# Two-pair attention stack on one core: key weights on SyncE's queue, two tiles centred by ScalarE, five packed tiles instead of seven

## The chip, the cores and the metric

The kernel runs on one core of one Trainium2 chip. The metric is the device time of one execution in microseconds (us); the median of three executions of the kernel before is 408.18 us (407.64 to 408.44). A profiled execution, the one that the trace describes, took 409.25 us, of which 407.40 us lie between its first and its last instruction (the span).

## The reference

Four residual layers run over 2048 rows of 512 features, 32 heads of 16 features each, in bf16. Layers A and B alternate, with the same weights both times: A, B, A, B.

```python
phi = lambda t: jnp.where(t > 0, t + 1, jnp.exp(t)) + 1e-6      # layer A
kv  = einsum("bhsd,bhse->bhde", phi(k), v);  z = sum over s of phi(k)
o   = (phi(q) @ kv) / (phi(q) . z + 1e-6)
scores = q @ k.T * Dh ** -0.5                                    # layer B
mask   = (i - j >= 0) & (i - j < 256)                            # each row sees itself and 255 before it
o      = softmax(where(mask, scores, -1e9)) @ v
x = x + A(layernorm(x)); x = x + B(layernorm(x)); and both again
```

## The kernel before

The rows are cut into T = 16 tiles of 128, kept in SBUF from the first load to the last store. The engines: PE is TensorE, ACT ScalarE, DVE VectorE, POOL GpSimd, SP SyncE (it only issues DMAs).

A tile is normalised in `norm`: `stats` and `aggr` (mean and variance) on DVE, `eps` and `pow` (the variance to the power of -0.5, into `rs`) on POOL, then `xn` on DVE subtracts the mean and multiplies by `rs`. The result is transposed into `XQ`, for the first five tiles by PE (`T`, then a copy `Te` out of PSUM by ACT or DVE), for the others by a transposing DMA of SP. From the transposed tile PE makes keys (`k`, four matmuls of 512 columns in two halves `h`, each with two of the four row blocks of the weights `wA[:, :, 512:1024]`) and, for pairs of tiles, queries (`q`). `phi` finishes keys and queries: ACT takes the exponential (`E`), DVE clips it (`E1`), and then either DVE adds one and takes the larger straight from PSUM (`phi`, L451 in the profile), or ACT makes a copy with the one added (`R`, L446) and DVE takes the larger from SBUF (`mx`, L449). In the first layer PE also sums `g`, the product of the normalised tile with its keys.

Layer B works per tile j with keys `kB` against 256 + 64 query columns in blocks of 64 keys: `b_scores` (`s`, L710 on PE, L720 on ACT: the exponential of 128 x 1024 scores) and, for the 64 columns at the window's far end, `b_far` (L826 on PE, two exponentials of 128 x 1024 each, L835, and two masks `mf`, L806 on POOL or L807 on DVE). A packed tile (`PACK`) starts its 256 columns 32 later and takes the two remaining corners of 32 columns together in `b_edge` (L779 on PE, two exponentials of 128 x 512 each, L788, one more mask `ma` on DVE, L794), so that it computes 288 columns instead of 320. Then `pv` (L856) multiplies by the values, and `rcp`, `div` finish the rows.

The order is not made by a scheduler at run time. `place` unpacks `TABLE`, which holds the order of all operations, the engine of those that two engines can do (copies out of PSUM, masks `mf`, stores), and the PSUM bank of each result. Every engine plays its own list in that order and waits on semaphores where an operand comes from another engine, so an instruction that waits holds up all behind it on its engine. PE starts with matmuls on zeros (nine in `play`, seven `fill` in the table) until the first data are there. The first x tiles come on SP's queue, the key weights on ACT's.

## Time and profile before

| | |
|---|---|
| median of 3 runs | 408.18 us (407.64 to 408.44) |
| profiled execution | 409.25 us, span 407.40 us, mean granted TensorE clock 0.998 |
| busy, share of the span | PE 95%, ACT 86%, DVE 86%, POOL 31% |
| first layer (keys of all tiles) | to about 44 us |
| second layer | about 50 to 225 us |
| third layer's sums and queries | about 225 to 256 us |
| fourth layer | about 250 to 395 us, last store behind it |

A PE that is busy 95% of the span is not one that could give no more: its matmuls are pipelined, and the time of one covers its latency. What it waits for is read from the gaps between the starts of its instructions, and from the chain of work that ended last, which the page follows back from the last instruction.

### The profile page before, as it was taken

The numbers are of one execution on the slowest core, as the hardware profiler recorded it, in microseconds if no ns is written. First come the engines' busy times: TensorE is split into PE (matmuls) and PEld (weight loads), VectorE is DVE, ScalarE is ACT, GpSimd is POOL, SyncE is SP. The second block draws the span as 40 slices with busy tenths as digits, with TensorE's granted clock in tenths as the row PEclk, the third lists the DMA queues.
The fourth block names the chain that finished last, engine by engine and source line by source line (L and its number), as shares of the span: only waits on it lengthen the run. The fifth ranks groups of instructions, "written<-read, shape, count | busy, mean of one in ns | idle before, by whom it ended". The sixth has DMA issues, their size and how long they took to land.

```text
span 407.4 us, 17007 instructions
## 1 busy us (share of the span) xinstructions
PE 386.1 (95%) x7394; PEld 255.7 (63%) x7466; DVE 349.3 (86%) x818; ACT 350.4 (86%) x447; POOL 125.8 (31%) x215
## 2 busy tenths in 40 slices
PE   7999999999999999999999999999999989998996
PEld 3644576667475567565656767676656756666674
DVE  5998899999999899888877799998899689777674
ACT  2843559999999999999999368999999999999992
POOL 3588752122243142331602122301203241320130
PEclk9999999999999999999999999999999999999999
DMA  7546324443233425553222100562324433572551
GB/s 253 138 113 163 98 42 107 101 101 81 68 101 78 91 82 121 80 108 80 77 49 56 27 2 2 121 122 69 80 55 101 119 89 68 111 142 77 85 148 40
DMA packets 66986, 37.15 MB, mean 91 GB/s; under 512 B 47648, under 2 KB 62368, under 8 KB 66912
## 3 DMA queue, kind: packets, MB, share of 16 engines
q1 hardware_dynamic: 66080, 34.75, 36.8%
q8 instruction: 59, 0.97, 1.1%
q0 software_dynamic: 288, 0.79, 0.5%
q10 hardware_dynamic: 544, 0.52, 0.4%
q14 instruction: 15, 0.12, 0.1%
HBM read 6.29 MB, written 2.10 MB: 21 GB/s over the span
## 4 chain that ended last, share of the span: by engine, by line
PE 54%; ACT 21%; DVE 14%; issue 5%; DMA 3%; POOL 1%; SPq 1%; POOLq 0%; DVEq 0%
PE ps L420 19%; ACT pb L720 16%; PE ps L856 11%; PE ps L434 8%; PE ps L710 6%; PE ps L480 4%; DVE stats L374 2%; ACT pb L835 2%; PE ps L524 2%; DVE XQ L625 2%; ACT vp L720 2%; DMA xres<-in_A_x_dram 1%; DVE xres L638 1%; DVE vp L451 1%; PE ps L826 1%
## 5 line engine op out<-in xcount | busy, mean ns | idle before, releaser
L720 ACT ACTIVATE pb<-ps 128x1024 bf16<-128x1024 f32 (+2 forms) x216 | 199.4, 1021 | 3.6 <-PE ps L710 2.4
L856 PEld LDWEIGHTS ps<-vB,pb 128*128 128x128 bf16 x2560 | 78.6, 96 | 11.4 <-issue 3.6
L856 PE MATMUL ps<-vB,pb 128*128 128x34 bf16 x2560 | 84.4, 177 | 0.3
L806 POOL TENSOR_SCALAR_AFFINE_SELECT pb<-pb 128x1024 bf16<-128x1024 bf16 x33 | 37.9, 1150 | 106.0 <-DVE pb L807 40.1
L434 PE MATMUL ps<-xT,wBp 128*128 128x128 bf16 x1024 | 69.6, 219 | 0.9 <-ACT pb L720 0.5
L434 PEld LDWEIGHTS ps<-xT,wBp 128*128 128x128 bf16 x1024 | 59.2, 98 | 13.3 <-issue 4.7
L444 ACT ACTIVATE tE<-ps 128x512 bf16<-128x512 f32 x64 | 37.8, 606 | 24.4 <-PE ps L420 9.9
L379 POOL TENSOR_SCALAR ve<-mv 128x1 f32<-128x1 f32 x63 | 16.4, 260 | 130.3 <-DVE mv L375 128.4
L710 PE MATMUL ps<-XQ,kB 32*128 32x256 bf16 (+3 forms) x992 | 48.1, 267 | 3.0 <-DVE o L869 0.5
L420 PE MATMUL ps<-wA,XQ 128*128 128x512 bf16 x175 | 45.3, 379 | 1.7 <-issue 0.5
L638 DVE TENSOR_TENSOR xres<-ps,xres 128x512 bf16<-128x512 f32 x63 | 42.8, 683 | 4.7 <-PE ps L420 4.2
L374 DVE BATCH_NORM_STATS2 stats<-xres 128x6 f32<-128x512 bf16 x64 | 43.2, 681 | 4.0 <-DMA xres<-in_A_x_dram 3.5
L728 DVE TENSOR_TENSOR pb<-pb,tri 128x512 bf16<-128x512 bf16 (+1 forms) x108 | 43.0, 407 | 3.8 <-ACT pb L720 2.9
L380 POOL TENSOR_TENSOR rs<-ve,negh 128x1 f32<-128x1 f32 x64 | 40.3, 630 | 7.6 <-DVE ve L377 2.4
L835 ACT ACTIVATE pb<-ps 128x1024 bf16<-128x1024 f32 x40 | 39.4, 1054 | 1.1 <-PE ps L826 1.1
L480 PE MATMUL ps<-XQ,wA 128*128 128x256 bf16 x256 | 34.1, 273 | 0.4 <-ACT pb L720 0.4
L710 PEld LDWEIGHTS ps<-XQ,kB 32*128 32x128 bf16 x992 | 15.0, 92 | 28.8 <-ACT pb L720 7.6
L420 PE MATMUL ps<-M,XQ 128*128 128x512 bf16 x113 | 30.5, 380 | 2.4 <-issue 0.6
L420 PE MATMUL ps<-wBv,xT 128*128 128x512 bf16 x109 | 30.3, 380 | 2.3 <-issue 1.4
L420 PE MATMUL ps<-wBo,oT 128*128 128x512 bf16 x107 | 28.9, 380 | 2.6 <-DVE tE L447 0.7
L869 DVE TENSOR_TENSOR o<-ps,rc 128x256 bf16<-128x256 f32 x64 | 27.0, 423 | 1.6
L480 PEld LDWEIGHTS ps<-XQ,wA 128*128 128x128 bf16 x256 | 23.6, 98 | 7.5 <-ACT pb L720 0.8
(132 smaller groups left out, 543.8 us busy)
## 6 DMA issues: line engine op xcount, KB each, us to landing
vB<-vS SPq DMA_DIRECT2D x64, 136.0 KB, 2.5
kB<-vp SPq DMA_DIRECT2D x60, 128.0 KB, 2.1
out_dram<-xres SPq DMA_DIRECT2D x9, 128.0 KB, 2.2
wA<-in_A_wqkv_dram SPq DMA_DIRECT2D x2, 512.0 KB, 5.5
xres<-in_A_x_dram SPq DMA_DIRECT2D x2, 512.0 KB, 4.0
pb<-in_B_wqkv_dram SPq DMA_DIRECT2D x1, 1024.0 KB, 6.6
xres<-in_A_x_dram SPq DMA_DIRECT2D x3, 256.0 KB, 5.5
out_dram<-xres POOLq DMA_DIRECT2D x6, 128.0 KB, 2.6
```

Source lines behind the costliest of these rows:

```text
L374: self.on("DVE", "stats", lambda e: e.bn_stats(K.stats[:, t, :], x()), key, dve(512), rd=rd, wr=[("stats", t)], **held)
L380: self.pow = self.on("POOL", "pow", lambda e: e.tensor_tensor(K.rs[:, t, :], K.ve[:, t, :], K.negh[:], ALU.pow), key + 0.03, (640, 690), r ...
L420: m = e.matmul(K.ps(ps), lhs(c), rhs(c), start=c == 0 and not whole, stop=c == 3)
L434: m = e.matmul(K.ps(ps)[:, f * P:(f + 1) * P], w(c, f), xT(c), start=c == 0, stop=c == 3)
L480: m = e.matmul(K.ps(ps)[:, 256 * h:256 * h + 256], K.wA[:, c, f * P:(f + 1) * P], xT(c), start=c == 0, stop=c == 3)
L638: self.on("DVE", "res", lambda e: e.tensor_tensor(K.xres[:, t, :], K.ps(po), K.xres[:, t, :], ALU.add), key, dve(512), rd=[("xres", t)], w ...
L710: m = e.matmul(K.ps(ps[gq])[:, ns * i:ns * i + ns], K.kB[rows, j % 4, 2 * f + b, :, :], K.XQ[rows, f, q:q + ns], start=True, stop=True, ti ...
L720: return e.activation(out(2 * h, 2, ns), i, ACT.Exp, bias=0.0, scale=0.25)
L728: return e.tensor_tensor(x, x, K.tri[:, 0, sh:64].unsqueeze(1).unsqueeze(1).to_broadcast([P, 4, n, 64 - sh]), ALU.mult)
L806: return e.affine_select(out=x, in_=x, compare_op=ALU.is_ge, fill=0.0, base=-2, pattern=[[0, 16], [-2, 64]], channel_multiplier=1)
L835: return e.activation(far(h), i, ACT.Exp, bias=0.0, scale=0.25)
L856: m = e.matmul(K.ps(ps)[:, 34 * u:34 * u + 34], K.P((b // 2) % rp)[:, gq, f, o:o + P], K.vB[:, (b // 2) % 4, b % 2, r, :], start=i == 0, s ...
```

## The change

It does seven things.

1. The two halves of the key weights (`wAk0`, `wAk1`, 256 KB each) are loaded by SP, between the loads of x; ACT issues one small DMA of 1 x 4 x 128 elements in their place, whose completion SP waits for ahead of the first `kd` (the DMAs that fill `kB` in layer B).
2. Tiles 0 and 1 (`CENTRED`) are centred by ACT (`xc`: mean minus x) without waiting for `rs`. PE transposes the centred tile in two halves, each copied out of PSUM with its sign turned, and makes the keys from it; `rs` enters as the scale of `E` and of `R`. The normalised tiles are still made by DVE, and `XQ` of these two tiles now comes by transposing DMAs of SP.
3. The keys of tiles 0 to 7 of the first layer (`KEYS_BY_ACT`) are finished with `R` on ACT and `mx` on DVE instead of `phi` on DVE.
4. Five tiles of the fourth layer are packed instead of seven: tiles 7 and 8 now go through `b_far`.
5. `TABLE` is a new one: order, engines and banks. Beside what the edits ask for, nine more of the 56 masks `mf` are POOL's (44 instead of 35), ACT has three copies of values (`ve`) instead of five, and single copies (`bke`, `bve`, `bqe`, `sc`, `ge`) change engine; the copies out of PSUM of the transposed tiles 3 and 4 are DVE's.
6. POOL's constants (masks, spreading matrices, reordered weights) come later in the first layer, behind more of the `eps` and `pow`.
7. The x tiles 8 to 15 are loaded behind the transposes of tiles 0 and 1.

```diff
-PACK = {3: (7, 8, 9, 10, 11, 12, 13, )}
+PACK = {3: (9, 10, 11, 12, 13, )}
+CENTRED = (0, 1)
+KEYS_BY_ACT = (0, 1, 2, 3, 4, 5, 6, 7)
...
-        seq += [xs(0, 1), xs(1, 2), w("wAq", "wA", "A_wqkv", 0, 512), xs(2, 4), xs(4, 6), xs(6, 8), xs(8, 12)]
+        def wk(h):
+            return ("wAk%d" % h, lambda e: e.dma_start(K.wA[:, 2 * h:2 * h + 2, 512:1024], ...), 262144, [("wAk", h)])
+        seq += [xs(0, 1), wk(0), wk(1), xs(1, 2), w("wAq", "wA", "A_wqkv", 0, 512), xs(2, 4), xs(4, 6), xs(6, 8), xs(8, 12)]
...
+        if centred:
+            self.on("ACT", "xc", lambda e: e.activation(K.xn[:, t, :], x(), ACT.Identity, bias=K.mv[:, t, 0:1], scale=-1.0), ...)
+            for h in range(2):
+                half = Tile(1, K.cls)
+                ...  # two transposes of K.xn, 128 columns each
+                self.pe("T", put, key + 0.018 + 0.0001 * h, 2, 128, rd=[("xn", t), ("ident",)], ps=[half])
+                self.either("Te", ... ACT.Copy, scale=-1.0 ... wr=[("xT", t, h)] + ([("xT", t)] if h else []), ps=[half])
+            by_pe = False
...
-    def phi(self, ps, out, wr, key, ring, near=False, after=()):
+    def phi(self, ps, out, wr, key, ring, near=False, after=(), row=None):
+        scale = lambda: dict(scale=K.rs[:, row, :]) if row is not None else {}
+        own = [("rs", row)] if row is not None else []
...
+        xT = (lambda c: K.xT[:, t, c, :]) if centred else (lambda c: K.XQ[:, c, t * P:(t + 1) * P])
+        self.phi(ps, lambda: K.pk[:, t, :], [("pk", t)], key + 0.1, 0, near=t in KEYS_BY_ACT and key < 150, row=t if centred else None)
...
-                    e.wait_ge(wsem, 1)
-                    for h in range(2):
-                        e.dma_start(self.wA[:, 2 * h:2 * h + 2, 512:1024], ...).then_inc(ksem[h], 16)
+                    e.dma_start(self.kB[0:1, 3, 0:4, :, :]..., self.A_wqkv...[0:1, :, 0:128]).then_inc(tsem, 16)
```

The new order is best seen at three places. The first is the head of SP's queue; `xres` is x, `wA` with 128x2x512 is a half of the key weights, `wA` with 128x4x512 the query weights, `pb` the weights of layer B. Before:

```order
L294 DMA xres<-in_A_x_dram 128x512 x2
L294 DMA xres<-in_A_x_dram 128x2x512 x3
L297 DMA wA<-in_A_wqkv_dram 128x4x512
L294 DMA xres<-in_A_x_dram 128x4x512 x2
L389 DMA_TRANSPOSE XQ<-vp 128x4x128 x2
L297 DMA pb<-in_B_wqkv_dram 128x4x1024
```

And now:

```order
L297 DMA xres<-in_A_x_dram 128x512 x2
L297 DMA xres<-in_A_x_dram 128x2x512 x2
L303 DMA wA<-in_A_wqkv_dram 128x2x512 x2
L297 DMA xres<-in_A_x_dram 128x2x512
L300 DMA wA<-in_A_wqkv_dram 128x4x512
L410 DMA_TRANSPOSE XQ<-vp 128x4x128 x2
L297 DMA xres<-in_A_x_dram 128x4x512 x2
```

Both key halves stand behind the loads of tiles 0 to 5, and the last two x loads moved behind two transposes, which belong to tiles 0 and 1. The second place is the head of PE's list, where `kB` stands for the matmuls on zeros, `ident` for transposes and `wA` with 128x512 for keys. Before:

```order
L277 MATMUL ps<-kB 128x512 x4
L395 MATMUL ps<-ident,vp 128x128 x4
L277 MATMUL ps<-kB 128x512
L395 MATMUL ps<-ident,vp 128x128 x4
L277 MATMUL ps<-kB 128x512
L420 MATMUL ps<-wA,XQ 128x512 x4
L395 MATMUL ps<-ident,vp 128x128 x4
L420 MATMUL ps<-wA,XQ 128x512 x8
```

And now:

```order
L280 MATMUL ps<-kB 128x512 x4
L395 MATMUL ps<-ident,xn 128x128 x8
L280 MATMUL ps<-kB 128x512 x2
L441 MATMUL ps<-wA,xT 128x512 x4
L416 MATMUL ps<-ident,vp 128x128 x4
L441 MATMUL ps<-wA,xT 128x512 x4
L416 MATMUL ps<-ident,vp 128x128 x4
L441 MATMUL ps<-wA,XQ 128x512 x2
```

The transposes of both centred tiles now stand together ahead of the keys, and read what ACT wrote (`xn`), not what DVE wrote (`vp`). The first four key matmuls are the first halves of both tiles. The third place is ACT's list in the fourth layer, around the exponentials of the far columns of tiles 7 and 8 (128x8x2x32 for a packed tile, 128x8x2x64 for another). Before:

```order
L720 ACTIVATE pb<-ps 128x2x2x256 x8
L788 ACTIVATE vp<-ps 128x8x2x32 x2
L835 ACTIVATE pb<-ps 128x8x2x64 x2
L720 ACTIVATE pb<-ps 128x2x2x256 x6
L835 ACTIVATE pb<-ps 128x8x2x64 x2
L720 ACTIVATE vp<-ps 128x2x2x256 x6
L720 ACTIVATE pb<-ps 128x2x2x256 x2
L720 ACTIVATE vp<-ps 128x2x2x256 x2
L788 ACTIVATE pb<-ps 128x8x2x32 x2
```

And now:

```order
L743 ACTIVATE pb<-ps 128x2x2x256 x8
L858 ACTIVATE vp<-ps 128x8x2x64 x2
L858 ACTIVATE pb<-ps 128x8x2x64 x2
L743 ACTIVATE pb<-ps 128x2x2x256 x6
L858 ACTIVATE pb<-ps 128x8x2x64 x2
L743 ACTIVATE vp<-ps 128x2x2x256 x6
L743 ACTIVATE pb<-ps 128x2x2x256 x2
L743 ACTIVATE vp<-ps 128x2x2x256 x2
L858 ACTIVATE pb<-ps 128x8x2x64 x2
```

Nothing changed places there; two pairs of exponentials became twice as long.

## The prediction

> **What bounds the kernel now.** I read the page's busy times, then the busy times in stretches of 10 us, then the chain of waits in order of time, then the engines' timelines where the change works. In the table by stretches, the columns are the stretch, its length, and the busy time of PE, PEld, DVE, ACT and POOL with counts, then clock, DMA share and GB/s:

> ```profile
> PE 386.1 (95%) x7394; PEld 255.7 (63%) x7466; DVE 349.3 (86%) x818; ACT 350.4 (86%) x447; POOL 125.8 (31%) x215
> 0.00:10.00 10.00, 7.89 (x32) 3.06 (x33) 5.41 (x15) 2.48 (x3) 3.27 (x14) 1.00 0.78 253
> 20.00:30.00 10.00, 9.89 (x65) 4.84 (x64) 9.92 (x30) 5.12 (x9) 8.31 (x17) 1.00 0.48 120
> 160.00:170.00 10.00, 9.78 (x213) 6.63 (x212) 8.71 (x23) 9.61 (x12) 1.70 (x4) 1.00 0.61 84
> 370.00:380.00 10.00, 9.01 (x303) 7.37 (x300) 7.14 (x20) 9.85 (x13) 0.00 (x0) 1.00 0.37 85
> ```

> PE and a second engine are full nearly everywhere, and the second changes: DVE in the first layer (9.92 of 10 at 20 to 30 us, ACT only 5.12), ACT later (9.85 at 370 to 380, with PE at 9.01). So one microsecond of ACT work is nearly free in the first layer and nearly a microsecond of time in the last. The chain of waits says the same (start, length, what):

> ```profile
> 1.72 5.19 DMA xres<-in_A_x_dram
> 27.72 0.58 DVE vp L451
> 28.35 1.04 PE ps L420 x4
> 342.08 3.77 ACT pb L720 x4
> ```

> Until 28.3 us the chain runs through the load of tiles 2 and 3, which ends at 6.91, and then mostly through DVE; from there PE and ACT carry it.

> **First layer, start.** PE's timeline (start, length, what, and the idle time before it):

> ```profile
> 6.77 0.40 PE L395 MATMUL ps<-ident,vp 128*128 128x128 bf16 x4
> 8.21 0.40 PE L395 MATMUL ps<-ident,vp 128*128 128x128 bf16 x4 [0.81 <-DVE vp L381]
> 8.65 1.24 PE L420 MATMUL ps<-wA,XQ 128*128 128x512 bf16 x4
> 9.73 0.39 PE L395 MATMUL ps<-ident,vp 128*128 128x128 bf16 x4
> 9.96 1.89 PE L420 MATMUL ps<-wA,XQ 128*128 128x512 bf16 x8
> 11.68 0.39 PE L395 MATMUL ps<-ident,vp 128*128 128x128 bf16 x4
> ```

> The matmuls on zeros end at 6.77 in both kernels. Then PE transposes tile 0, and waits for DVE to normalise tile 1, which stood behind `stats` of tile 2, that is, behind the load that ended at 6.93; the keys begin at 8.65. Start to start, four transposes take 0.23 (9.73 to 9.96) and eight key matmuls with no wait 1.72 (9.96 to 11.68), 0.215 each. In the new order, 6.77 is followed by eight transposes (0.46) and two matmuls on zeros (0.43), so keys could begin at 7.66, **1.0 earlier**. Three things must be there by then:

> ```profile
> 2.89 0.69 DVE L374 BATCH_NORM_STATS2 stats<-xres 128x6 f32<-128x512 bf16 x1 [1.69 <-DMA xres<-in_A_x_dram]
> 4.62 0.18 DVE L375 BATCH_NORM_AGGREGATE mv<-stats 128x2 f32<-128x6 f32 x1
> 7.21 0.60 ACT L402 ACTIVATE XQ<-ps 128x512 bf16<-128x512 bf16 x1 [3.68 <-PE ps L395]
> L407 ACT ACTIVATE oT<-ps 128x256 bf16<-128x256 bf16 x2 | 0.8, 384 | 3.2 <-PE ps L894 3.2
> L446 ACT ACTIVATE XQ<-ps,one 128x512 bf16<-128x512 f32 x12 | 8.1, 693 | 0.1
> ```

> Centred tiles: the means of both tiles are ready at 4.80 (4.62 + 0.18); two passes of about 0.69 on ACT (`xc` has the operands of `R`, L446) end at 5.5 to 6.2, before 6.77. Copies: the first half-transpose gives its copy at about 7.1, and a copy of 256 columns takes 0.38, so the first key matmul can start at 7.5 and the fourth copy ends at 8.6, while the second halves of the keys are due at 8.7. Key weights: 253 GB/s over the first 10 us are 2.53 MB; with hardly a byte there before 2 us (the first `stats` waits for its tile until 2.89) that is an estimated 315 GB/s. Behind 0.79 MB of x on SP's queue the halves are complete after 1.05 and 1.31 MB, at about 5.3 and 6.2. All three fit, with 2 us to spare for the weights and only 0.1 for the copies.

> **First layer, feeding.** The gaps that PE still has:

> ```profile
> 27.27 2.12 PE L420 MATMUL ps<-wA,XQ 128*128 128x512 bf16 x8
> 29.27 1.04 PE L524 MATMUL ps<-vp 128*128 128x512 bf16 x4
> 30.36 0.81 PE L420 MATMUL ps<-wA,XQ 128*128 128x512 bf16 x3
> ```

> Eight matmuls are 1.72, so 27.27 to 29.27 holds 0.28 of waiting; the next four are 0.86, so 29.27 to 30.36 holds 0.23; with 0.22 before 9.73 that is 0.73, all on DVE. DVE's own load sinks:

> ```profile
> L451 DVE SCALAR_TENSOR_TENSOR vp<-ps,tE 128x512 bf16<-128x512 f32 x32 | 21.5, 682 | 0.4
> L449 DVE TENSOR_TENSOR XQ<-XQ,tE 128x512 bf16<-128x512 bf16 x12 | 5.0, 421 | 0.0
> L402 DVE COPY xT<-ps 128x512 bf16<-128x512 bf16 x1 | 0.4, 407 | 0.0
> 6.93 0.69 DVE L374 BATCH_NORM_STATS2 stats<-xres 128x6 f32<-128x512 bf16 x1 [1.83 <-DMA xres<-in_A_x_dram]
> ```

> Eight keys at 682 - 421 ns save 2.1 us, two more copies cost 0.8, and with x ahead of the weights tiles 2 and 3 are there (0.52 MB) at about 3.7 instead of 6.9, so DVE's 1.83 us of idling before 6.93 go too. That is 3.1 us of DVE in 21. ACT pays 8 x 0.69 for `R` and two centrings, 6.9 us, where it was half idle; the cover is its idle 4.9 us of 10 at 20 to 30, thinner before. I take **-0.45** of the 0.73, for POOL's and SP's turns are not gone, and -1.45 for the layer. Bounds: -1.75 if no gap is left, 0 if new waits eat the lead.

> [...]

> **What is moved on SP.** `x8` and `x12` (1 MB) now wait behind two transposes, which wait for DVE to normalise tiles 0 and 1. Before, they were issued at 6.93 and about 9.9:

> ```profile
> 6.93 3.32 SPq L294 DMA_DIRECT2D xres<-in_A_x_dram  x2
> 13.93 2.92 SPq L389 DMA_TRANSPOSE XQ<-vp  x2
> ```

> By the new list DVE reaches tile 0's `xn` behind six `stats` (0.69 each from 2.89) and some 2.2 of smaller passes, at about 9.2; that transpose holds SP for 1.46, so I estimate that `x8` is issued at 10.9 and, with the 3 us that 0.5 MB take with their start, lands near 14. DVE is due to take its `stats` at about 15.5, an estimate from the passes ahead of it. Cost 0, hidden by 1.5 us; beyond that each microsecond delays tiles 8 to 15.

> **Second layer.** ACT gives two copies to DVE in a stretch where it has no pause:

> ```profile
> 156.81 0.75 ACT L661 ACTIVATE vp<-ps 128x512 bf16<-128x512 f32 x1
> 170.37 0.70 ACT L407 ACTIVATE vS<-ps 128x512 bf16<-128x512 f32 x1
> ```

> These are 1.45 us where both ACT and PE are nearly full (9.61 and 9.78 of 10). If only ACT counts, -1.45; if PE, 0. I take **-0.7**.

> **Fourth layer.** Tiles 7 and 8 lose their packing. ACT's and PE's rows there:

> ```profile
> 319.98 1.08 ACT L788 ACTIVATE vp<-ps 128x512 bf16<-128x512 f32 x2 [0.39 <-PE ps L779]
> 321.30 1.94 ACT L835 ACTIVATE pb<-ps 128x1024 bf16<-128x1024 f32 x2 [0.23 <-PE ps L826]
> 333.35 3.77 ACT L720 ACTIVATE vp<-ps 128x1024 bf16<-128x1024 f32 x4 [0.59 <-PE ps L710]
> 340.81 1.08 ACT L788 ACTIVATE pb<-ps 128x512 bf16<-128x512 f32 x2
> 319.29 0.61 PE ps L779 x64
> 320.87 0.34 PE ps L826 x32
> ```

> A pair of large exponentials takes 1.94 (321.30), a pair of small ones 1.08 (319.98), so a tile pays 0.86 on ACT; on PE it gains 0.61 - 0.34 = 0.27. Tile 7's falls at 320, where ACT idled 0.39 + 0.23 + 0.59 = 1.2 within 14 us: absorbed. Tile 8's falls at 340.8, and from 342.08 the chain is ACT's: **+0.9**. Bounds: -0.55 (PE sets the pace), +1.7 (ACT does, throughout).

> **Masks.** Nine `mf` go from DVE to POOL:

> ```profile
> L806 POOL TENSOR_SCALAR_AFFINE_SELECT pb<-pb 128x1024 bf16<-128x1024 bf16 x33 | 37.9, 1150 | 106.0 <-DVE pb L807 40.1
> L807 DVE TENSOR_TENSOR pb<-pb,tri 128x1024 bf16<-128x1024 bf16 x17 | 11.9, 706 | 0.0
> ```

> 9 x 0.71 = 6.4 us leave DVE, 9 x 1.15 = 10.4 fall on POOL, which had 31%. What could show is a `pow` queued behind a mask: 0, bounds -0.5 and +0.5.

> **Sum.** -1.45 - 0.7 + 0.9 = -1.25 on a span of 407.40; the profiled execution would take 408.0 instead of 409.25. The median lies 1.07 below the profiled one, so 408.18 - 1.25 = **406.9 us**. A measurement of this kernel can tell about 0.2%, 0.82 us, from no change: faster means below 407.36, slower above 409.0.

> **Rivals.**
> - *Everything pays* (chance 0.17): -1.75 in the first layer, -1.45 in the second, +0.4 in the fourth, sum -2.8, 405.4 us. For it: PE's gaps are all DVE's. Against it: ACT and PE are both full in the second layer, so a copy less shows only in part.
> - *The lead is not kept* (0.15): the load order doesn't bring x earlier or the weights come after 8.7, or `x8` lands after 15.5; the first layer gives 0, the rest +0.2: 408.4 us. Against it: 2 us of room for the weights.
> - *ScalarE becomes the bound* (0.20, the slower side): in the first layer each key's PSUM bank is now freed by `E` and `R`, two passes on ACT, and PE's keys and sums wait for banks; in the fourth the packing goes. Eight passes of 0.69 are 5.5; if a quarter of that, 1.4, shows, the lead of 1.0 turns into +0.4; the fourth layer gives +1.7, the second still -0.7: +1.4, 409.6 us. It decides from the point where ACT is busy without a pause from 8 to 24 us, so that PE's banks come free at ACT's rate. For it: ACT is already at 8.4 of 10 in the second stretch:

> ```profile
> 10.00:20.00 10.00, 9.95 (x75) 6.64 (x74) 9.93 (x31) 8.39 (x16) 5.50 (x14) 1.00 0.52 130
> ```

> - *My forecast* (0.48), 406.0 to 407.8 by itself.

> **Numbers.** Faster: 0.17 and most of 0.48 (0.43); same: 0.05 of it and the lost lead; slower: ScalarE. The range, 405.3 to 409.5, leaves out half of the slower case, around its 409.6, and the best of the good one, around its 405.4.

> **What would show it.** Right: first key matmul at 7.5 to 7.8, `stats` of tile 2 near 4.7, the keys and `g` of all tiles done by 42.5 instead of 44, the chain of the first layer on PE and not on DVE; ACT still full at 340 to 390, its far exponentials of tiles 7 and 8 at 2 x 1.0 instead of 2 x 0.5. Wrong: a key matmul that waits for the weights' DMA or for ACT's copies after 8.6, PE idle before `q` for the transposes of tiles 0 and 1, `xn` waiting for POOL in the last two layers; a fourth layer longer by more than 1.7 would overturn the sum.

## The result, and the profile after

The changed kernel takes 410.38 us (median of 12 executions, 408.86 to 413.41) against 408.37 us (12 executions of the kernel before on the same chip, 407.43 to 409.94): a ratio of **1.0038 [1.0021, 1.0056]**, slower by 0.38%, where 406.9 us was forecast. Later on, 17 more executions of the same kernel gave 1.0037 and 1.0039. Four executions of all that follow fell into a slower state (three with a mean clock of 0.56 to 0.85, and one of the kernel before, 413.71 us at 0.996) and are left out of every ratio and mean.

The profiled execution took 409.7 us, its span is 407.8 us. Busy times and the chain that ended last, from the page of the changed kernel:

```profile
PE 385.0 (94%) x7333; PEld 254.5 (62%) x7402; DVE 346.1 (85%) x814; ACT 355.7 (87%) x452; POOL 134.7 (33%) x225
...
PE 50%; ACT 27%; DVE 14%; issue 4%; DMA 3%; POOL 1%; POOLq 0%; DVEq 0%
```

The work moved as the prediction said: DVE lost 3.2 us, ACT gained 5.3, POOL 8.9, PE lost 1.1. The opening did too. PE's timeline of the changed kernel (start, length, what, idle time before it):

```profile
6.20 0.59 PE L280 MATMUL ps<-kB 128*128 128x512 bf16 x2
7.09 1.04 PE L441 MATMUL ps<-wA,xT 128*128 128x512 bf16 x4 [0.30 <-ACT xT L399]
...
8.24 1.04 PE L441 MATMUL ps<-wA,xT 128*128 128x512 bf16 x4
...
10.69 0.40 PE L416 MATMUL ps<-ident,vp 128*128 128x128 bf16 x4 [0.76 <-DVE vp L402]
```

Keys begin at 7.09 instead of 8.65, before the forecast 7.5 to 7.8 (at 7.85 and 7.61 in two later profiles of the changed kernel), and the chain's first stretch waits for x until 2.90 instead of 6.91. But the profile of before was an unlucky one. A second profile of the unchanged kernel, PE's timeline at the same place:

```profile
7.58 1.24 PE L420 MATMUL ps<-wA,XQ 128*128 128x512 bf16 x4
8.66 0.39 PE L395 MATMUL ps<-ident,vp 128*128 128x128 bf16 x4
```

The same program starts its keys 1.07 earlier here and keeps 1.27 of lead from 44 us on. So I compared several profiles. I matched the same VectorE instructions in each trace (the last copy of `g` at 44 us, the reciprocals of later rows) and took their times against the first profile of before; the end is the span less the reciprocal at 391 us. This table is worked out from the traces, not a view:

```
             44 us   57     122    181    250    304    345    391  | end    span
before          0     0      0      0      0      0      0      0     16.34  407.4
  again     -1.27 -1.27  -1.27  -1.25  -1.18  -1.18  -1.17  -1.60     16.36  405.8
changed     -1.06 -1.24  -1.19  -0.43  -0.02  +0.17  +0.30  -0.38     17.07  407.8
  again     -1.07 -1.25  -1.19  -0.82  -1.03  -0.84  -0.45  -0.72     18.64  409.0
  third     -1.10 -1.28  -1.08  -0.63  -0.84  -0.63  +0.15  -0.58     16.55  407.0
```

The means of three and of two profiles differ by 407.92 - 406.61 = +1.31 us: **-0.62 up to 57 us, +0.58 from 57 to 250, +0.28 from 250 to 391, +1.07 behind 391**. Two thirds of the 2.0 us between the medians are in these profiles. The largest piece is the end. PE's timelines there, of before, of the changed kernel and of its second profile:

```profile
397.37 0.24 PE L710 MATMUL ps<-XQ,kB 32*128 32x64 bf16 x8
```

```profile
397.00 0.23 PE L733 MATMUL ps<-XQ,kB 32*128 32x64 bf16 x6
397.88 0.20 PE L733 MATMUL ps<-XQ,kB 32*128 32x64 bf16 x2 [0.65 <-issue]
```

```profile
397.07 0.23 PE L733 MATMUL ps<-XQ,kB 32*128 32x64 bf16 x6
398.39 0.20 PE L733 MATMUL ps<-XQ,kB 32*128 32x64 bf16 x2 [1.09 <-issue]
...
402.08 0.63 PE L441 MATMUL ps<-wBo,oT 128*128 128x512 bf16 x1 [0.22 <-issue]
```

A group of eight score matmuls runs whole before; after, PE stops inside it, behind six, and waits for nothing that the profile shows ("issue"). That what it lacks there is the rest of its program is my reading of the counts below. The page of the changed kernel, DMA queues (packets, MB, share), and the whole-kernel view of the transposing DMAs' line:

```profile
q8 instruction: 58, 0.95, 1.0%
```

```profile
DMA to landing us min/median/max: 2.3/2.5/5.1
```

```profile
oT<-o SPq DMA_TRANSPOSE x1, 5.1
```

```profile
oT<-o SPq DMA_TRANSPOSE x1, 5.3
```

Both land twice as late as the median, at 397.77 and 398.27, and PE goes on 0.11 and 0.12 later. That nearness is no proof that PE waits for them. Two counts over all the profiles of this case speak for the packet instead. In the nine profiles that have PE's records complete (e9 to e12 and e14 to e18 below, whose counts differ by just the instructions that their edits add or take), eleven idle times of PE of 0.25 us and more behind 50 us end at "issue"; counted from the first instruction, all eleven end at place 193, 194 or 195 of a block of 256. And in all profiles together there are 20 such stops, of 0.26 to 1.09 us; in each PE goes on 1.26 to 1.53 us after the end of a fetch packet, and in five of them no transposing DMA is in flight while the packet passes.

What followed this stop is shown by stretches of 1 us of the second profile (columns as in the prediction):

```profile
397.00:398.00 1.00, 0.30 (x9) 0.11 (x6) 0.68 (x2) 0.51 (x2) 0.00 (x0) 1.00 0.03 4
398.00:399.00 1.00, 0.57 (x17) 0.50 (x18) 0.00 (x0) 0.36 (x2) 0.00 (x0) 1.00 0.00 0
399.00:400.00 1.00, 0.94 (x30) 0.76 (x27) 0.43 (x1) 0.30 (x2) 0.00 (x0) 0.85 0.06 16
400.00:401.00 1.00, 1.00 (x42) 1.00 (x39) 0.43 (x2) 0.00 (x0) 0.00 (x0) 0.50 0.00 0
401.00:402.00 1.00, 0.86 (x31) 0.80 (x29) 0.69 (x3) 0.00 (x0) 0.00 (x0) 0.50 0.00 0
402.00:403.00 1.00, 0.92 (x6) 0.64 (x6) 0.83 (x3) 0.04 (x1) 0.00 (x0) 0.50 0.00 0
```

From about 1.3 us behind the stop on, the granted clock is 0.50 for 3.4 us: the end takes 18.64 instead of 16.34. Of 29 executions of the changed kernel, 13 have a mean clock below 0.997 (mean time 411.04, the other 16: 409.47); of 109 of the kernel before, 5 (410.94, the others: 408.35). By these means, 409.47 - 408.35 = 1.1 us of the loss are there at the full clock, and 13/29 of 1.57 less 5/109 of 2.59 = 0.6 us come with the low ones. Where the clock fell is seen in one of the 13 alone, the one that was profiled.

### The profile page after: what moved, and what is told of

It reads as the page before. It is cut to its first block, busy times and chain, and to the rows that moved or that the text cites. A ratio compares the mean times of both kernels' runs of the same rounds, so it can differ in the third digit from the quotient of the medians.

```text
span 407.8 us, 16913 instructions
## 1 busy us (share of the span) xinstructions
PE 385.0 (94%) x7333; PEld 254.5 (62%) x7402; DVE 346.1 (85%) x814; ACT 355.7 (87%) x452; POOL 134.7 (33%) x225
## 4 chain that ended last, share of the span: by engine, by line
PE 50%; ACT 27%; DVE 14%; issue 4%; DMA 3%; POOL 1%; POOLq 0%; DVEq 0%
ACT pb L743 19%; PE ps L441 18%; PE ps L455 8%; PE ps L879 7%; PE ps L503 5%; PE ps L733 4%; PE ps L547 3%; ACT pb L858 3%; ACT vp L743 3%; DVE stats L380 2%; DMA XQ<-xn 2%; DVE xres L661 1%; DVE XQ L648 1%; DVE pb L751 1%; DVE xn L402 1%
## 5 line engine op out<-in xcount | busy, mean ns | idle before, releaser
L829 POOL TENSOR_SCALAR_AFFINE_SELECT pb<-pb 128x1024 bf16<-128x1024 bf16 x39 | 45.3, 1161 | 93.4 <-DVE pb L751 39.6
L751 DVE TENSOR_TENSOR pb<-pb,tri 128x512 bf16<-128x512 bf16 (+1 forms) x108 | 43.4, 410 | 4.6 <-ACT pb L743 4.3
L661 DVE TENSOR_TENSOR xres<-ps,xres 128x512 bf16<-128x512 f32 x63 | 43.0, 685 | 4.8 <-PE ps L441 4.1
L441 PE MATMUL ps<-wA,XQ 128*128 128x512 bf16 x168 | 43.5, 379 | 2.7 <-DMA XQ<-xn 0.6
L858 ACT ACTIVATE pb<-ps 128x1024 bf16<-128x1024 f32 x42 | 41.1, 1051 | 0.8 <-PE ps L849 0.6
L386 POOL TENSOR_TENSOR rs<-ve,negh 128x1 f32<-128x1 f32 x64 | 37.8, 590 | 5.3 <-DVE ve L383 0.2
L441 PE MATMUL ps<-wBv,xT 128*128 128x512 bf16 x110 | 31.2, 380 | 2.3 <-issue 0.9
L891 DVE RECIPROCAL rc<-ps 128x16 f32<-128x16 f32 x64 | 16.1, 252 | 14.5 <-PE ps L879 13.6
```

The costliest lines, as they stand in the source:

```text
L386: self.pow = self.on("POOL", "pow", lambda e: e.tensor_tensor(K.rs[:, t, :], K.ve[:, t, :], K.negh[:], ALU.pow), key + 0.03, (640, 690), r ...
L441: m = e.matmul(K.ps(ps), lhs(c), rhs(c), start=c == 0 and not whole, stop=c == 3)
L661: self.on("DVE", "res", lambda e: e.tensor_tensor(K.xres[:, t, :], K.ps(po), K.xres[:, t, :], ALU.add), key, dve(512), rd=[("xres", t)], w ...
L751: return e.tensor_tensor(x, x, K.tri[:, 0, sh:64].unsqueeze(1).unsqueeze(1).to_broadcast([P, 4, n, 64 - sh]), ALU.mult)
L829: return e.affine_select(out=x, in_=x, compare_op=ALU.is_ge, fill=0.0, base=-2, pattern=[[0, 16], [-2, 64]], channel_multiplier=1)
L858: return e.activation(far(h), i, ACT.Exp, bias=0.0, scale=0.25)
```

## The experiments

**The parts apart.** Four kernels carry the changed order, engines and edits over a part of the program, and those of before over the rest.

```diff
e1_opening_only:   -TABLE = order of before      +TABLE = changed to 44 us, then as before (7 packed tiles)
e2_middle_only:    -TABLE = order of before      +TABLE = as before to 44 us, changed to 240 us, then as before
e3_last_only:      -PACK = {3: (7, ..., 13)}     +PACK = {3: (9, ..., 13)}, and the changed order from the fourth layer on
e8_last_as_before: -PACK = {3: (9, ..., 13)}     +PACK = {3: (7, ..., 13)}, and the order of before from the fourth layer on
```

> The opening of the changed kernel (key weights by SyncE in two loads, two centred tiles, keys of eight tiles from a ScalarE copy, and its order on every engine up to the last key matmuls of the first layer), then the order, the engines and the seven packed tiles of the kernel before. Nothing of the computation is left out. Theory L (the lead of the opening is real, about 1.07 us in the profile, and it is lost later to something that the change put there): 1.0 to 1.1 us below the kernel before, ratio 0.997 to 0.998. Rival D (the lead is taken away anyway by a later wait on a transfer that does not come earlier, as after the transposes by DMA near 183 us): within 0.4 us of the kernel before, ratio 0.999 to 1.001. Rival O (the opening itself is what is slower in most runs, and the profiled run was a lucky one): 1.5 to 2 us above, ratio 1.004 to 1.005.

> The opening and the last layer of the kernel before; between the end of the first layer and the start of the fourth the order and the engines of the changed kernel (copies moved from ScalarE to VectorE, masks from VectorE to GpSimd). Nothing is left out. Theory L with the loss in the middle: 1 us above the kernel before, ratio 1.002 to 1.003, since the lead of 1.0 us went between 167 and 200 us in the profiled pair. Rival D: within 0.3 us, ratio 0.999 to 1.001. My prediction's term for the two moved copies would be 0.7 us below, ratio 0.998.

> All of the kernel before up to the start of the fourth layer; there five tiles of 288 columns instead of seven, and the order and the engines of the changed kernel. Nothing is left out. Theory L with the loss in the last layer: 1.5 to 3 us above the kernel before, ratio 1.004 to 1.007 (the part of the 2.0 us that the profiled pair does not show in the middle). My prediction's term: 0.9 us above, ratio 1.002. Rival (five and seven tiles cost the same, as the profiled pair has it, 132.25 us against 131.77 us): within 0.5 us, ratio 0.999 to 1.001.

> The changed kernel itself once more, on the chip of the three others, so that the three parts can be summed against it. Its median so far stands 2.0 us above the kernel before. If the parts are independent, its distance to the kernel before is the sum of the three others' distances; a rest of more than 0.7 us would be an effect that only the parts together have.

Measured: opening 1.0035 [1.0021, 1.0049], middle 1.0064 [1.0040, 1.0087], last layer 1.0015 [0.9996, 1.0034], everything (the changed kernel again) 1.0037 [1.0023, 1.0052]. The parts add up to +4.6 us, the whole is +1.35: nothing here can be added. The opening alone had a lead of 0.99 at 44 us and lost it at my own seam, where the two orders meet (PE's timeline of that kernel):

```profile
45.12 1.07 PE L562 MATMUL ps<-kB,wA 128*128 128x128 bf16 x16 [0.71 <-DVE rec L626]
```

So it says nothing on the opening. The middle alone loses 0.83 from 57 to 250 us and 0.48 at the end, which runs as before there.

> The kernel before, unchanged, for a second profiled execution. Its first profile (409.25 us) lies 1.0 us above the median of its runs (408.25 us). If the opening is what differs between runs of it, as the two mixed kernels with its opening suggest (the last key copies of the first layer at 43.2 us less 0.82 in one, plus 0.06 in the other), this profile ends near 406.4 us of span, with the copies 0.8 us earlier than in the first profile and the rest of the way the same. If the opening is as in the first profile and the gain is elsewhere, the lead of 1.07 us that the changed kernel had there stands.

Measured: 407.54, span 405.8. This is the second profile of before shown above: the opening of before can be as early as the changed one. Over six profiles of programs with the opening of before, `g` at 44 us stands at 0, -1.27, -0.82, +0.06, -1.39 and -1.00, mean -0.74; over 13 with the changed opening the mean is -0.90, and eleven of them lie between -0.89 and -1.11. The changed opening is steadier, and about 0.2 us earlier.

> The changed kernel up to the start of the fourth layer, there the seven tiles of 288 columns, the order and the engines of the kernel before. Nothing is left out. If five tiles in place of seven and the new order of the last layer are what costs, 1 us below the kernel before (407.2 to 407.6 us), the lead of the opening kept. If the lead is lost ahead of the last layer, or what is lost at the end is the same here, 408.2 to 409 us. If the last layer is not the cause at all, as the changed kernel, 409.6 to 410.4 us.

Measured: 1.0042 [1.0018, 1.0067]. With all seven packed tiles back, the time stays as long, so the work of the two unpacked tiles is not what is paid; but the loss has another place here. Its profile has a stop like that of the end, at another place, inside the corners of tile 7:

```profile
340.98 0.66 PE L802 MATMUL ps<-XQ,kB 32*64 32x32 bf16 x62
342.65 0.20 PE L802 MATMUL ps<-XQ,kB 32*64 32x32 bf16 x2 [1.01 <-issue]
```

**Does it hang on where the blocks' borders fall?** From here on I tested a theory of my own, made from the packets and stops above: that PE's program arrives in blocks of 256 instructions, that a fetch and a transposing DMA delay each other, and that it depends on the count of instructions ahead which ones meet. The first pair adds 126 PE instructions at the start, without adding work:

```diff
-for _ in range(9):  e.matmul(self.PS[:, SPARE, :], warm[:, 0:P], warm, ...)
+for _ in range(72): e.matmul(self.PS[:, SPARE, 0:64], warm[:, 0:P], warm[:, 0:64], ...)
```

> The changed kernel with the nine warming products of 512 columns at the very start split into seventy-two of 64 columns: the same columns, on the same data that no result reads, but TensorE's program is 126 instructions longer ahead of everything else. Nothing is left out. Theory F (at the end TensorE stands 0.65 to 1.1 us in the middle of a group of products, waiting for nothing but its own next instructions, which it fetches in blocks of 256; the place of the block's border decides it; the halved clock that follows in half of the runs costs 1.3 us more): the border moves off the last scores, the stall near 397 us falls below 0.5 us, runs with a granted clock under 0.997 (9 of 18 so far) become rare, and the median falls by 0.7 to 1.3 us, to 408.7 to 409.2 us. Rival S (the end is late because of the changed order there, its masks and its output transfers): the stall or another wait of the same length stays, the median stays at 409.6 to 410.4 us.

> The kernel before with the same split of the warming products, so that its program's borders move by 126 instructions the other way round: the border that lies some 400 instructions ahead of the end comes to some 275, near where the changed kernel has its own. Nothing is left out. Theory F: a stall of 0.5 to 1.1 us appears near 397 us, runs with a clock under 0.997 (1 of 19 so far) become common, the median rises by 0.7 to 1.3 us to 409.0 to 409.5 us. Rival S: nothing changes, 408.0 to 408.5 us.

Measured: 1.0139 [1.0118, 1.0160] for the changed kernel, 1.0105 [1.0078, 1.0133] for before. The shift removed the stop at the end (16.47), and cost 5.4 us between 57 and 250; in before it made no stop at the end (16.16), a miss, and 3.1 us between 57 and 250. Where it went: PE's timeline and the DMA's issue (KB, us from issue to landing) of the shifted kernel, then both of the changed kernel unshifted:

```profile
76.53 0.62 PE L455 MATMUL ps<-xT,wBp 128*128 128x128 bf16 x8 [1.31 <-DMA xT<-xn]
```

```profile
xT<-xn SPq DMA_TRANSPOSE x1, 4.6
```

```profile
74.58 0.61 PE L455 MATMUL ps<-xT,wBp 128*128 128x128 bf16 x8
```

```profile
xT<-xn SPq DMA_TRANSPOSE x1, 2.7
```

Issued at 71.89, the transposition lands at 76.49, with a fetch from 73.99 to 74.94 inside; unshifted, issued at 71.39, it lands at 74.09 with none.

The next three were meant to act on the end alone: one-column matmuls, two instructions each with the weight load, ahead of it in the changed kernel (e9), and in the kernel before, to bring the stop there (e10); and the last-but-two tile's `o` transposed by PE and copied by DVE, so that no transposing DMA is in flight at the end (e11).

```diff
e9_after_border:   +DUMMY = {7: 3, ..., 12: 3}
e10_before_border: +DUMMY = {7: 3, 8: 3, 9: 2, ..., 12: 2}
+for _ in range(DUMMY.get(j, 0) if K.rp == 4 else 0):
+    e.matmul(K.ps(ps)[:, 504:505], K.ident[:], K.ident[:, 0:1], ...)
e11_one_less_dma:  -LAST = {2: 1, 3: 2}   +LAST = {2: 1, 3: 3}
```

> The changed kernel with 72 more products of one column, three ahead of each of the 24 products of P and V of tiles 7 to 12 of the fourth layer, into columns of the bank that nobody reads: 144 more instructions of TensorE between 325 and 385 us, about 2.0 us of its time at 28 ns each, mostly in its waits there. Two tiles fewer of 288 columns had taken 146 instructions out of that stretch, so that the last borders of its blocks of 256 came to lie some 260 instructions ahead of the end (96 instead of 146 and 402 in the kernel before is meant by this: 262 against 146 and 402); now they lie at 150 and 406 again. Theory F (the stall of 0.65 and 1.1 us at 397 us, and the halved clock after it, come from that border together with the transposition by DMA that is under way there until 398 us): no stall above 0.3 us near 397 us, hardly a run under a clock of 0.997, median 0.3 to 1.3 us below the changed kernel, 408.7 to 409.6 us, the added products included. Rival S (the order at the end is at fault): stall or another wait stays, 409.8 to 411 us.

> The kernel before with 56 such products more (three ahead of each product of P and V of tiles 7 and 8, two in tiles 9 to 12), 112 instructions, so that its last borders come from 146 and 402 instructions ahead of the end to 258 and 514, where the changed kernel has them. Theory F: the stall of 0.5 to 1.1 us appears near 397 us, and runs under 0.997 become common; median 0.7 to 2 us above the kernel before, 409 to 410.3 us, of which the added products by themselves are at most 0.7 us. Rival S: only the added products are paid, 408.2 to 408.9 us, and the end takes the 16.34 us from the last division of tile 15 that it takes in both profiles of the kernel before.

> The changed kernel; the attention output of tile 13 in the fourth layer is transposed by TensorE (and copied back by VectorE) instead of by DMA, as those of tiles 14 and 15 are already. It is the transposition that is issued at 392.7 us and lands at 397.8 us in the first profile, 0.07 us before TensorE's stall ends. Theory F: with no transposition under way the block of instructions that is asked for at 392.2 us comes in time, the stall goes, the clock stays up; 0.5 to 1.5 us below the changed kernel, 408.4 to 409.4 us. Rival S, or if the output transfers of 128 KB hold the fetch: the stall stays, 409.6 to 410.6 us.

Measured: 1.0067 [1.0046, 1.0087], 1.0078 [1.0049, 1.0108], 1.0029 [1.0004, 1.0054]. e9 and e10 did not do what their texts say. A group of instructions in e9's profile and one place in its PE timeline:

```profile
L876 PE MATMUL ps<-ident 128*128 128x1 bf16 x144 | 10.5, 165 | 0.0
```

```profile
145.30 0.22 PE L876 MATMUL ps<-ident 128*128 128x1 bf16 x3
```

The condition on `K.rp` holds in the second layer too. So e9 has 144 matmuls more and not 72, half of them between 145 and 202 us, and e10 has 112 instead of 56. They lost 2.1 and 1.8 us between 57 and 250 us, nearly all of it behind 122 us, in the stretch where the added matmuls stand. Sixteen one-column matmuls take 0.41 us in the changed kernel's PE timeline (41.97 to 42.38), so 72 and 56 of them are an estimated 1.8 and 1.4 us; the two medians say nothing about the end. The counts move the border too. The last border stands 243 instructions ahead of the end in the changed kernel and 135 in the kernel before. e10, with 224 more, has it at 103 and not where the changed kernel has it; its end took 16.50 without a stop, so the stop that it was to make was not made, and the theory was not tried by it. e9, with 288 more, has borders 276 and 20 ahead of the end, and e14 (below) has them at the same places with 32 more and no added work.

At the end itself the changed kernel took 16.10 (e9) and 16.60 (e11) instead of 17.42 in the mean, with no stop at "issue" of 0.25 us or more, and 1 and 2 of 12 executions had a clock below 0.997 instead of 13 of 29. e11 leaves the border where it was, at the same pair of scores, and its PE still stands there for 0.3 us (397.19 to 397.48). But so does the third profile of the changed kernel (e16, 396.83 to 397.13), which has the transposing DMA in flight. So one profile of e11 does not show that it is the missing DMA that made the stop short.

The opening again, with the seam at 91 us, and the same with ten instructions more at the start:

```diff
e12_opening_to_91:  -TABLE = order of before   +TABLE = changed to 91 us, then as before (7 packed tiles)
e13_seam91_plus10, e17_plus10_again:  -range(9) of 512 columns   +range(14) of 329 columns
```

> As the first experiment, but with the seam at 91 us instead of 44 us, at a place where both kernels have run the same operations, so that no wait is made by the seam: all of the changed kernel up to there, and from there the order, the engines and the seven tiles of the kernel before. If the opening gains 0.6 us over the mean opening of the kernel before (as the two profiles of each have it) and what follows is independent of it, 0.3 to 1.0 us below the kernel before, 407.2 to 407.9 us. If any other place of the fetched blocks against the transpositions costs more than that (which the two shifted kernels showed with 3 to 5 us), it comes out above the kernel before in spite of the gain, 408.5 to 411 us, and the profile shows transpositions with a fetch inside them on which TensorE waits.

> The mixed kernel of the twelfth experiment (changed up to 91 us, as before from there), with its nine warming products split into fourteen of the same columns together, so that TensorE's program is 10 instructions longer ahead of everything. The changed opening had made it 10 instructions shorter (15166 against 15176); with them the borders of the fetched blocks lie where the kernel before has them. Nothing is left out. Theory F: the stall of 1.0 us inside the 64 small products of tile 7 near 341 us, which this kernel showed and the kernel before does not, goes; the median falls from 409.9 by 0.7 to 1.3 us, to 408.6 to 409.2 us. Rival S (the stall comes from the order): it stays within 0.2 us of 1.0 us, the median at 409.6 to 410.2 us.

> The thirteenth experiment once more, for a profile that can be set beside the others: its own was taken in an execution whose TensorE ran at 0.755 of its clock throughout. Theory F: no stall over 0.3 us near 341 us inside the 64 small products of tile 7 of the fourth layer, where the same kernel without the 10 instructions stood 1.02 us; about 409 us. Rival S: it stands 0.8 to 1.1 us there.

Measured: 1.0042 [1.0016, 1.0068] for e12, 1.0028 [1.0000, 1.0055] with ten more (e13), 409.97 for the one execution of e17, the same kernel as e13. Tile 7's corners in PE's timeline of e12, and then of e17, and a line of e17's waits of PE (us in total, times, longest):

```profile
339.55 0.67 PE L802 MATMUL ps<-XQ,kB 32*64 32x32 bf16 x63
341.25 0.20 PE L802 MATMUL ps<-XQ,kB 32*64 32x32 bf16 x1 [1.02 <-issue]
```

```profile
339.60 0.68 PE L802 MATMUL ps<-XQ,kB 32*64 32x32 bf16 x64
```

```profile
PE ps L441 <- DMA oT<-o: 1.7, 2, 1.4
```

In e12 a packet passes from 338.61 to 339.79 and PE stops 1.02 us; ten instructions more, and the packet passes from 337.09 to 338.01 and the group runs whole. That is the clearest test here: the same columns of work, ten instructions more 330 us earlier, and a stop of 1 us goes. No transposing DMA is in flight while e12's packet passes, so this stop needs none. It was not a gain of 1 us: between 345 and 391 us e17 gives 0.86 back, waiting for two transposing DMAs (the last line above).

> The changed kernel with the nine warming products split into 25 of the same columns together: 32 instructions more ahead of everything, no other work. Nothing is left out. Theory F: the block that comes late at 397 us is asked for 32 instructions earlier, ahead of the wait at 391.5 us and of the last transposition by DMA (392.7 us); no stall over 0.3 us in the last 15 us, at most 2 runs in 12 under a clock of 0.997, and the end takes 16.1 to 16.6 us from the last division of tile 15 instead of 17.1 and 18.7. What the rest of the way does is open: borders that move by 32 can meet other transpositions; 408.7 to 410.5 us. Rival S: the end stays at 17.1 us or more.

```diff
e14_after_plus32:  -range(9) of 512 columns   +range(25) of 184 columns
```

Measured: 1.0103 [1.0059, 1.0146]. The end took 16.20, as expected; but 5 of 6 executions had a clock below 0.997, and the body was late. Its PE timeline and that DMA's issue, then the same DMA in the changed kernel:

```profile
135.13 1.59 PE L441 MATMUL ps<-wBo,oT 128*128 128x512 bf16 x4 [2.29 <-DMA oT<-o]
```

```profile
oT<-o SPq DMA_TRANSPOSE x1, 5.0
```

```profile
oT<-o SPq DMA_TRANSPOSE x1, 3.3
```

A fetch from 132.01 to 133.91 lies in the flight of the first, and PE stands for 2.29 us; its next four matmuls take 1.59 instead of 1.04, with the granted clock at 0.50 from 135.5 us on, for 3.4 us (a mean of 0.83 over 130 to 140 us): in this profile it fell behind a wait for a DMA, not behind a stop at "issue".

**A wait in the opening.** The 0.76 us ahead of 10.69 come from `xn` of two tiles, 1.67 us on DVE while POOL clears a value buffer. I moved that clearing behind the `pow` of tile 4.

```diff
e15_after_memset_later:  -POOL: c21, ..., pow 4   +POOL: ..., pow 4, c21
```

> The changed kernel with one thing moved on GpSimd: the first clearing of the value buffer (1.02 us at 9.47 us) goes behind the power of tile 4 and the clearing of the ones. In the profile VectorE's two normalisations there take 1.67 us together instead of 0.76 us and TensorE waits 0.76 us for them at 10.69 us. Nothing is left out. If the changed opening is bound there by VectorE and GpSimd and not by the key weights, the last key copies of the first layer come 0.4 to 0.8 us earlier than in the changed kernel (lead 1.5 to 1.9 us over the first profile of the kernel before instead of 1.06 us), and the end as far as transpositions let it. If the clearing only moves to hold up other work of VectorE, no change (within 0.2 us).

Measured: 1.0052 [1.0025, 1.0078]. The two `xn` took 0.88 and PE's transposes came at 10.17 without a wait; by 20 us the half microsecond was gone (21.60 against 21.76), and at 44 us the lead was 1.07, as in the changed kernel. From 15 to 45 us PE is busy 29.79 of 30 us here: the wait removed ahead of that stretch bought nothing by itself.

**The best of it together.**

```diff
e18_one_less_dma_plus10:  e11 with range(14) of 329 columns
```

> The changed kernel once more, for its distance to the two variants above on the same chip, and a third profile of it: 409.5 to 410.5 us; a third to a half of the runs under a clock of 0.997; lead at the end of the first layer 1.0 to 1.1 us unless the transfers of the start come in another order; the end 17 us or more.

> The changed kernel with both amendments that lowered a time: tile 13's output transposed by TensorE in the fourth layer (409.56 us by itself) and 10 more instructions ahead, so that up to the fourth layer the borders of the fetched blocks lie as in the kernel before (0.65 us less in the thirteenth experiment against the twelfth). Nothing is left out. Theory F: at the end no stall over 0.4 us, between 57 and 250 us a loss of 0.1 to 0.4 us as in most profiles of the kernel before, instead of the 0.4 to 1.2 us of the changed kernel's profiles; 408.4 to 409.3 us, within 0.3% of the kernel before and below the changed kernel. Rival S: 409.3 to 410.3 us, as with the first amendment alone.

Measured: 1.0039 [1.0014, 1.0064] for the changed kernel a third time (the third profile above), 1.0032 [1.0009, 1.0055] for e18. As expected the end had no long stop (16.62), the body lost only 0.29 between 57 and 250, and 1 of 12 executions had a low clock. But 304 to 345 us lost 0.89, with a stop of 0.48 at 343.37 in another group of scores. No version here beats the kernel before.

## Why the prediction was wrong

Three steps of the sum failed: the opening was mis-sized (-1.45), the second layer's -0.7 did not come, and no term stood for what came on top, stops of PE at "issue", read here as late blocks of its program, and waits for DMAs that landed late.

**Opening: -1.45 forecast, -0.44 to -0.62 found against two profiles of before, about -0.2 over all.** What the edits set going came as described: x earlier, both tiles centred while `rs` is still made, `stats` of tile 2 at 4.74, the chain of this layer mostly on PE, keys and `g` done about 1.1 earlier than in the first profile of before (`g` to 43.4, where 42.5 was named). Both parts of the size failed.

The first, -1.0, took 8.65 for the normal start of the keys, though the text itself said that this execution lay 1.07 above the median. The unchanged kernel starts at 7.58 when its x tiles come on time. I should have read those 1.07 as sitting in a wait of that one profile, and the first candidate, `stats` waiting 1.83 for x, was among my own rows.

The second, -0.45 of 0.73 us of gaps, rested in part on a gap that is none. Behind 29.27 the prediction's row has three key matmuls where there are four: a record is missing, and its 0.23 us is that matmul. e10 has the same opening and its records complete:

```profile
28.28 1.04 PE L525 MATMUL ps<-vp 128*128 128x512 bf16 x4
29.15 1.03 PE L421 MATMUL ps<-wA,XQ 128*128 128x512 bf16 x4
```

And instead of losing gaps the changed layer got one, ahead of 10.69. Its keys began at 7.09, 7.85 and 7.61 in the three profiles, and all three stand at 10.65 to 10.69 with the same transposes and at 44 us within 0.04 of each other. From the first key to the last copy of `g` it took 36.35 us in the first profile, where before took 35.85 and 35.65: of the 0.49 us that its keys are ahead of before's second profile nothing is left at 44 us (0.21 behind).

**Second layer: -0.7 forecast, +0.58 found from 57 to 250 us.** Busy times in that stretch, of before and of the changed kernel:

```profile
57.00:250.00 193.00, 186.19 (x3544) 124.52 (x3583) 173.26 (x401) 175.94 (x220) 53.94 (x86) 1.00 0.34 77
```

```profile
57.00:250.00 193.00, 184.90 (x3533) 123.64 (x3567) 173.07 (x400) 173.20 (x215) 55.39 (x88) 1.00 0.35 79
```

ACT's work in this stretch went down by 2.7 us, of which an estimated 1.1 is only that the changed kernel got 1.22 us less far in it; the two copies (1.45) did leave ACT, and nothing became faster. PE is busy 186.19 and 184.90 of the 193 us, and the other bound of the step (0) fits; the runs don't show it apart. On top came longer waits of PE for transposing DMAs, which the prediction had no term for: one of 0.16 in both profiles of before, of 0.56, none and 0.58 in the three of the changed kernel. The first of them, its PE timeline and the issue (landing at 182.95, a fetch from 180.55 to 181.88 inside):

```profile
183.08 1.02 PE L441 MATMUL ps<-wA,XQ 128*128 128x512 bf16 x4 [0.56 <-DMA XQ<-xn]
```

```profile
XQ<-xn SPq DMA_TRANSPOSE x1, 4.4
```

**Fourth layer: +0.9 forecast, +0.28 up to 391 us and +1.07 behind it.** Busy times up to there, of before and of the changed kernel:

```profile
250.00:391.00 141.00, 133.89 (x3180) 93.32 (x3203) 117.20 (x272) 138.03 (x164) 33.03 (x51) 1.00 0.41 92
```

```profile
250.00:391.00 141.00, 134.25 (x3118) 92.43 (x3140) 114.12 (x267) 139.24 (x163) 40.04 (x56) 1.00 0.40 92
```

ACT's 1.2 us more and the fall of DVE by 3.1 with POOL's rise by 7.0 are the unpacked tiles and the masks; e3, with the changed fourth layer alone, is slower by 0.15% (0.6 us), with 1 in its interval, so the +0.9 is not refuted. The end was in no term. The change takes 146 PE instructions out (15,030 against 15,176 in all; 136 by the two tiles, 10 in the opening), so by this reading the borders of the last blocks fall at other instructions. That the stop comes from there and not from the tiles' own work is shown by e9 and e14, which keep the tiles, move the border by 32 instructions and lose the stop.

**Masks, x8 and x12, key weights.** Nothing in the traces shows a loss from them; they were not tried alone. `x8` was issued at 10.61 (10.9 forecast) and landed at 14.65: its 0.5 MB took 4.0 us, as they do in the page of before too, and not the 3 that the prediction estimated, and the 1.5 us of room covered that. The key weights came later than estimated, though: PE's weight loads of the changed kernel, with the wait ahead of the first key,

```profile
7.08 0.55 PEld L441 LDWEIGHTS ps<-wA,xT 128*128 128x128 bf16 x4 [0.79 <-DMA wA<-in_A_wqkv_dram]
```

so that the weights (estimated for 5.3 and 6.2) landed at 7.04 and 8.19, and the first held the first key at least as long as the copy that PE's row names (0.30). That is one of the signs that the prediction named as wrong; against its 7.5 it cost nothing.

**The rivals.** None was it. ScalarE as the bound gave the nearest time (409.6), by luck: ACT is busy 8.27 and 8.14 of 10 us at 10 to 20 and 20 to 30 us, not without a pause, and no wait of PE behind 7.09 us in this layer is for ACT's copies. The lost lead named the wrong signs (the weights came ahead of 8.7, `x8` ahead of 15.5), but against before's second profile its 0 for the first layer is nearer than -1.45. With ten more passes on ACT (6.9 us by the prediction) the changed kernel is at 44 us 1.06 to 1.10 earlier than the first profile of before and 0.17 to 0.21 later than the second.

**Shown, and not shown.** Shown: PE's stops of 0.25 us and more at "issue" stand at one place in 256 instructions (eleven of eleven, 193 to 195) and end 1.26 to 1.53 us behind a packet (all 20), and a shift of ten instructions took such a stop of 1.02 us away (e12, e17); a transposing DMA with a fetch in its flight landed after 3.28 us in the median, one without after 2.43, and PE waited for such a late one for 1.31 us in e6 and 2.29 in e14; the end's +1.07 is such a stop and, in one profile, the low clock behind it. Not shown: what a packet holds, and why a DMA lands later with one in its flight; that a transposing DMA in its turn makes a block late (e12's stop has none in its packet's flight, and at the end e16 with one stands as short as e11 without); why the changed order takes 0.1 to 1.2 us more from 57 to 250 us, in more waits than the ones named; and where the clock fell in the executions that were not profiled. Taking the end's stop away alone did not bring the kernel back to the time of before (e11, e18). A kernel with the changed work and no such stops and late landings at all was not reached, so what the seven edits would give without them stays open.

## What to carry over

Before a wait in one profile is priced, look at a second profile of the same kernel, above all where the first lies above the median: the keys of the unchanged program began at 8.65 us in one profile and at 7.58 in the other. Here edits that changed only how many instructions stand on TensorE, by 10 to 126, also changed where it stopped and which DMAs had a fetch in their flight, and that moved the time by 0.6 us (e12 to e13) to 4.3 us (e7) of 408 where the edits were worth one; so a gain of this size is tested with a few instructions more and fewer. Count an experiment's added instructions in its own trace before reading its time: e9 and e10 had twice as many as meant, half of them in another layer. And count the rows of a gap: behind 29.27 a missing record looked like a wait of 0.23 us. Two waits that a profile shows one behind the other need not add up: in e15 the wait of 0.76 us was gone, PE was full behind it, and the lead at 44 us stayed at 1.07.

## What was not expected of the hardware

- Over 19 profiles (all but e13's), 1350 transposing DMAs behind 52 us: with no fetch packet of PE's program in their flight they land after a median of 2.43 us (588, nine in ten within 2.62), with one after 3.28 (762, nine in ten within 4.22). It is not that a longer flight catches more fetches: counting only packets in the first 2.2 us after the issue, the medians are 2.44 and 3.40. In the kernel before, 40 of 71 are hit; what a change moves is which ones PE waits for.
- In the 20 stops at "issue" PE stood for 0.26 to 1.09 us, with no wait that the profile names, and went on 1.26 to 1.53 us behind the end of a fetch packet.
- The granted clock fell after little idle time: in the second profile a stop of 1.09 us, in two microseconds in which PE was busy for 0.30 and 0.57, was followed by a clock of 0.50 for 3.4 us. It did not always: e12's stop of 1.02 us was followed by 1.00. In e10's profile, whose longest stop at "issue" is 0.4 us, it fell too (a mean of 0.996); where, is not shown.
